# First batch's attention in halves of the tokens: turns, scores and softmax of two chunks of x while the other two land

## Chip, cores, metric

One core of one Trainium2 chip. The metric is the device time of the whole program in microseconds (us). A program on one core has no second core to compare states with; every run here was classed fast.

The profiles use short names: PE is TensorE (the array of products), PEld its weight loads, DVE VectorE, ACT ScalarE, POOL GpSimd, SP SyncE, which here issues transfers. L304 is line 304 of the kernel. The grant is the share of its full clock that the array is given. To turn a tile is to transpose it with a product on PE.

## The reference

Eight batches of a cross attention between 512 tokens and 32 state rows per head, then a feed-forward layer with the activation h * erf(softplus(h)) over 4608 rows in the reference's sizes (4352 come out: 8 x (512 + 32)).

```python
scores = scale * np.matmul(x, state.transpose(0, 1, 3, 2))     # x: 8,8,512,64  state: 8,8,32,64
scores = scores - scores.max(-1, keepdims=True)
a = np.exp(scores)
a /= a.sum(-1, keepdims=True) + 1e-09
xread = np.matmul(a, state)
# ... the same the other way round gives sread (32 rows a head); concatenated on the token axis
h = x2 @ w_in                                                  # 512 -> 2048
g = h * erf(np.maximum(h, 0.0) + np.log1p(np.exp(-np.abs(h))))
out = g @ w_out                                                # 2048 -> 512
```

Only the attention of batch 0, in the first 22 us, is touched by the change.

## The kernel before: the parts that matter

The transfers of the opening, in the order of their issue. Chunks 0 and 2 of x go out on ACT's queue, 1 and 3 on SP's; the state (`st`) follows on SP, then the first weights:

```python
x_t[0] = xin.tile([P, NC, H, D], F32, name="x")
for c in range(NC):
    (nc.scalar, nc.sync)[c % 2].dma_start(
        out=x_t[0][:, c], in_=x[0, :, P * c:P * c + P].rearrange("h p d -> p h d"))
for e in range(2):
    nc.sync.dma_start(out=st[:, 0, D * e:D * e + D],
                      in_=state[0].rearrange("(i e) n d -> e i n d", e=2)[e])
```

Dummy products keep the array busy (`warm`); `states` turns the state; instructions of each engine stay in the order in which they are written.

```python
def warm(n):
    for _ in range(n):
        last = nc.tensor.matmul(out=spare[:, 0:P], lhsT=ident, rhs=ident, start=True, stop=True)

# attention0, cut:
for c in 1, 0, 2, 3:
    if c == 2:
        warm(3)
    for i in range(NI):
        nc.tensor.transpose(out=xp[i][:, P * c:P * c + P],
                            in_=xt[:, c, 2 * i:2 * i + 2, :], identity=ident)
for i in range(NI):                       # all four chunks at once
    (nc.scalar.copy, nc.vector.tensor_copy)[i % 2](xT[:, i, :], xp[i])
states(range(1))
s2 = scored(0, xT)
between[0]()                              # warm(32), first weights on ACT
...
for e in range(2):                        # states_weights
    nc.vector.transpose(out=both[:, e], in_=sc[e])
for e in range(2):
    nc.vector.reduce_max(out=m1[:, e], in_=a[:, e], axis=AX.X)
for e in range(2):
    nc.vector.tensor_tensor(a[:, e], a[:, e], over(m1[:, e]), op=ALU.subtract)
    nc.scalar.activation(out=a[:, e], in_=a[:, e], func=ACTF.Exp, scale=scale)
# ... sums, conversion of the first weights (L147 to L149), normalise, transpose to aT, L703
```

Of the kernel before, what the change touches and what calls it, by code (L numbers as in the profile page):

```python
# [8 lines left out]
F32 = mybir.dt.float32  # L9
U32 = mybir.dt.uint32  # L10
ALU = mybir.AluOpType
ACTF = mybir.ActivationFunctionType
AX = mybir.AxisListType
# [3 lines left out]
def kernel(  # L17
# [17 lines left out]
    nc = tc.nc  # L35
    B, H, S, D = x.shape
    Ns = state.shape[2]
    d_model, d_ff = moe_w_in.shape
    P = 128
    NI = H // 2  # L40
    NC = S // P
# [5 lines left out]
    scale = 1.0 / (D ** 0.5)  # L47
# [4 lines left out]
    xin = ctx.enter_context(tc.tile_pool(name="xin", bufs=1))  # L52
    att = ctx.enter_context(tc.tile_pool(name="att", bufs=1))
    small = ctx.enter_context(tc.tile_pool(name="small", bufs=2))
    keep = ctx.enter_context(tc.tile_pool(name="keep", bufs=2))
# [3 lines left out]
    ps_at = ctx.enter_context(tc.tile_pool(name="ps_at", bufs=2, space=PSUM))  # L59
    ps_h = ctx.enter_context(tc.tile_pool(name="ps_h", bufs=2, space=PSUM))  # L60
    ps_o = ctx.enter_context(tc.tile_pool(name="ps_o", bufs=1, space=PSUM))

    ident = const.tile([P, P], F32, name="ident")
# [42 lines left out]
    st = const.tile([P, B, P], F32, name="st")  # L106
# [7 lines that stand above are left out]
# [52 lines left out]
    def warm(n):  # L166

        for _ in range(n):
            last = nc.tensor.matmul(out=spare[:, 0:P], lhsT=ident, rhs=ident, start=True,
                                    stop=True)  # L170
        return last
# [3 lines left out]
    aT = {}  # L175

    def states(bs):


        ps = ps_h.tile([P, len(bs), P], F32, name="h")  # L180
        for k, b in enumerate(bs):
            last = nc.tensor.transpose(out=ps[:, k], in_=st[:, b, :], identity=ident)
        nc.scalar.copy(st[:, bs[0]:bs[-1] + 1, :], ps)
        return last

    over = lambda t: t.unsqueeze(2).to_broadcast([P, NC * NI, Ns])
# [3 lines left out]
    def scored(b, xT):  # L190


        s2 = [ps_at.tile([P, S], F32, name="at") for _ in range(2)]
        for i in reversed(range(NI)):
            for e in range(2):
                r, q = slice(D * e, D * e + D), slice(Ns * i, Ns * i + Ns)
                on_pe = nc.tensor.matmul(out=s2[e][q, :], lhsT=st[r, b, q], rhs=xT[r, i, :],  # L197
                                         start=True, stop=True)
        marks.append(on_pe)
        return s2  # L200
# [10 lines left out]
    def states_weights(b, sc, both):  # L211

        aT[b] = keep.tile([P, 2, S], F32, name="aT")
        a = both[:, 0:2].rearrange("p e (k n) -> p e k n", n=Ns)
        m1 = small.tile([P, 2, NC * NI], F32, name="m1")
# [7 lines that stand above are left out]
        return a  # L223

    def sums(a):
        z1 = small.tile([P, 2, NC * NI], F32, name="z1")
        for e in range(2):
            nc.vector.reduce_sum(out=z1[:, e], in_=a[:, e], axis=AX.X)
        return z1

    def normalise(a, z1):
        nc.vector.tensor_scalar(z1, z1, 1e-9, None, op0=ALU.add)
        nc.vector.reciprocal(z1, z1)
        for e in range(2):
            nc.vector.tensor_tensor(a[:, e], a[:, e], over(z1[:, e]), op=ALU.mult)

    def largest(sc):
        m2 = small.tile([P, 2], F32, name="m2")
        for e in range(2):
            nc.vector.reduce_max(out=m2[:, e:e + 1], in_=sc[:, e], axis=AX.X)  # L240
        nc.vector.tensor_scalar(m2, m2, -scale, None, op0=ALU.mult)
        return m2

    def weigh_tokens(sc, m2, a2):

        z2 = small.tile([P, 2], F32, name="z2")
        for e in range(2):
            nc.scalar.activation(out=a2[:, e], in_=sc[:, e], func=ACTF.Exp, bias=m2[:, e:e + 1],
                                 scale=scale, accum_out=z2[:, e:e + 1])
        return z2  # L250

    def inverse(z):
        nc.vector.tensor_scalar(z, z, 1e-9, None, op0=ALU.add)
        nc.vector.reciprocal(z, z)

    def turn_weights(a2):
        a2T = att.tile([P, 2, NC, P], F32, name="sc")
        for e in range(2):
            ps = ps_at.tile([P, NC, P], F32, name="at")
            for c in range(NC):  # L260
                nc.tensor.transpose(out=ps[:, c, :], in_=a2[:, e, P * c:P * c + P],
                                    identity=ident)
            nc.scalar.copy(a2T[:, e], ps)
        return a2T
# [27 lines left out]
    def attention0(between):  # L292



        xt = x_t[0]
        xT = att.tile([P, NI, S], F32, name="xT")
        xp = [ps_o.tile([P, S], F32, name="o%d" % i) for i in range(3)]
        xp.append(ps_h.tile([P, S], F32, name="h"))
        for c in 1, 0, 2, 3:  # L300
            if c == 2:
                warm(3)
            for i in range(NI):
                nc.tensor.transpose(out=xp[i][:, P * c:P * c + P],  # L304
                                    in_=xt[:, c, 2 * i:2 * i + 2, :], identity=ident)
        for i in range(NI):
            (nc.scalar.copy, nc.vector.tensor_copy)[i % 2](xT[:, i, :], xp[i])
        states(range(1))
        s2 = scored(0, xT)
        between[0]()  # L310
        both = att.tile([P, NI, S], F32, name="xT")
        sc = att.tile([P, 2, S], F32, name="sc")
        a = states_weights(0, s2, both)
        for e in range(2):
            nc.scalar.copy(sc[:, e], s2[e])
        between[1]()
        z1 = sums(a)
        between[2]()
        normalise(a, z1)
        for e in range(2):  # L320
            nc.vector.transpose(out=aT[0][:, e], in_=both[:, e])

        def rest():
            a2 = both[:, 2:4]
            m2 = largest(sc)
            yield
            z2 = weigh_tokens(sc, m2, a2)
            inverse(z2)
            yield
            a2T = turn_weights(a2)  # L330
            yield
            read_tokens(0, a2T, z2)
            yield

        return rest()

    def turn_x(b):
        xT = att.tile([P, NI, S], F32, name="xT")
        last = nc.vector.transpose(out=xT.rearrange("p i t -> p (i t)"),
                                   in_=xq_t.pop(b).rearrange("p i m d -> p (i m d)"))  # L340
        if b + 1 < B:
            load_xq(b + 1)
        return xT, last
# [289 lines left out]
    def begins(b):  # L633
        return 1 - b % 2
# [44 lines left out]
    def fetch():  # L679
        if len(made) < len(pieces):  # L680
            kind, j = w = pieces[len(made)]
            made[w] = (weights_in if kind == "i" else weights_out)(j)

    def on_act(kind, j, ks=range(2)):
        for k in ks:
            made[kind, j][0][k]()

    def on_dve(kind, j, ks=range(3)):
        for k in ks:
            made[kind, j][1][k]()  # L690
            if k == 2:
                fetch()
# [25 lines left out]
    def group():  # L718
        return [act.tile([P, 4, S], F32, name=n) for n in ("s", "hs")]
# [3 lines left out]
        fetch()  # L723
    warm(8)

    def after_scores():
        warm(32)
        on_act("i", 0)

    def before_sums():  # L730
        on_act("i", 1)
        on_dve("i", 0, [0, 1])

    def amid_sums():
        on_dve("i", 0, [2])
        on_act("o", 0, [0])
        m_t[0, 0] = mix.tile([P, 2, gw], F32, name="m")
        mixed_part(0, 0, 0, 2, nc.scalar.copy, nc.scalar.copy)
        warm(5)

    rest = attention0((after_scores, before_sums, amid_sums))
    g0 = group()

    def some0(g, gT, rs, ts):
# [112 lines left out]
    xT, _ = turn_x(1)  # L857
# [7 lines left out]
    turn = attention(1, xT)  # L865
# [40 lines left out]
    at = [combine_a(1)]  # L906
# [12 lines left out]
    for b in range(1, B + 1):  # L919
# [4 lines left out]
        for g, (first, second) in enumerate(groups):  # L924
# [5 lines left out]
            if b + 1 < B:  # L930

                late = b == 1
                if g == late:
                    side[6 if late else 6] = (lambda: behind(marks, next, turn)) if late else \
                        lambda old=turn: (next(old), behind(marks, next, turn))
                    turn = attention(b + 1)
# [3 lines left out]
                if g > 1:  # L940
                    o = g - 2 ^ begins(b + 1)
# [56 lines left out]
```

## Time and profile before

| | before |
|---|---|
| time, median of 6 runs (range) | 734.82 us (734.64 to 735.06) |
| span of the profiled run, mean grant of the array's clock | 733.0 us, 0.999 |
| PE, DVE, ACT busy | 98%, 71%, 54% |
| first half transpose of the scores on DVE | 11.46 us |
| first L703 (first product with the attention weights) | 21.99 us |
| first projection | 30.87 us |

The last three rows are the ones to follow. The opening is a chain that ends in the first projection; after it PE works nearly without a gap. The prediction below shows the lines. What it doesn't show is the view of busy time by stretches: after the stretch and its length come the busy time of PE, PEld, DVE, ACT and POOL (with the number of instructions), the granted clock, the DMA share and GB/s. The kernel before, in two stretches of about 3.4 us that matter later:

```profile
4.70:8.15 3.45, 2.40 (x20) 1.98 (x19) 0.00 (x0) 0.00 (x0) 0.00 (x0) 1.00 1.27 252
8.15:11.55 3.40, 2.44 (x28) 1.24 (x26) 1.38 (x3) 1.30 (x4) 0.00 (x0) 1.00 1.05 393
```

PE is busy for 70% of the first and 72% of the second (2.40 of 3.45, 2.44 of 3.40), and the grant is full.

### The profile page before, as it was taken

To read this page: it belongs to the slowest core of one execution; us is meant where nothing else is said; L and a number is where in the kernel's file an instruction comes from. 1 tells how busy PE (TensorE), PEld (TensorE's weight loads), DVE (VectorE), ACT (ScalarE), POOL (GpSimd) and SP (SyncE) were. 2 spreads that over 40 slices of the span, in tenths; PEclk is the share of its full clock that TensorE was granted. 3 is DMA by queue.
4 is the path that set the end of the run, shared out by engine and by line. 5 is a ranking of instruction groups with operands and counts; after the bars stand their busy time and mean duration, and the time that the engine had idled before them with its cause. 6 is when DMAs were issued, how large, how long until landed. Compare 5 with 4: busy or idle time off the path is not lost.

```text
span 733.0 us, 12127 instructions
## 1 busy us (share of the span) xinstructions
PE 721.4 (98%) x5016; PEld 587.0 (80%) x5016; DVE 523.7 (71%) x765; ACT 397.0 (54%) x499; POOL 0.7 (0%) x6
## 2 busy tenths in 40 slices
PE   8899999999999999999999999999999999999998
PEld 7434435878889888988989888988898899999996
DVE  4987887998698666867587669866686756675423
ACT  4898894657455445754355445554565434443340
POOL 0000000000000000000000000000000000000000
PEclk9999999999999999999999999999999999999999
DMA  7587842331152201410061104220121000000001
GB/s 233 175 244 213 218 95 58 87 58 21 38 97 55 53 1 44 102 30 30 1 144 23 37 1 93 57 43 13 26 62 30 30 1 30 1 30 1 30 1 29
DMA packets 139166, 46.40 MB, mean 63 GB/s; under 512 B 126696, under 2 KB 130536, under 8 KB 139112
## 3 DMA queue, kind: packets, MB, share of 16 engines
q1 hardware_dynamic: 136840, 44.92, 24.7%
q10 hardware_dynamic: 2272, 0.72, 0.5%
q8 instruction: 39, 0.64, 0.4%
q14 instruction: 15, 0.12, 0.1%
HBM read 33.03 MB, written 8.91 MB: 57 GB/s over the span
## 4 chain that ended last, share of the span: by engine, by line
PE 87%; DVE 6%; ACT 2%; issue 1%; DMA 0%; SPq 0%; DVEq 0%; ACTq 0%
PE o L593 48%; PE h L487 26%; PE o L543 6%; PE at L401 2%; PE h L401 1%; PE h L703 1%; PE at L197 1%; PE at L415 1%; PE h L277 1%; DVE hs L495 1%; DVE raw L569 1%; DVE s L538 1%; DVE s L716 0%; DVE hs L710 0%; DMA out_dram<-ot 0%
## 5 line engine op out<-in xcount | busy, mean ns | idle before, releaser
L593 PE MATMUL o<-w_out,s 128*128 128x256 f32 x480 | 118.2, 380 | 0.9 <-DVE ot L603 0.5
L593 PE MATMUL o<-raw,hs 128*128 128x256 f32 x480 | 117.0, 382 | 0.0
L494 ACT ACTIVATE s<-hs 128x512 f32<-128x512 f32 x120 | 75.3, 630 | 76.1 <-DVE hs L495 75.7
L593 PE MATMUL o<-w_out,hs 128*128 128x256 f32 x480 | 114.0, 380 | 0.2 <-DVE hs L592 0.2
L593 PEld LDWEIGHTS o<-raw,hs 128*128 128x128 f32 x480 | 90.0, 190 | 22.5 <-issue 10.9
L495 DVE TENSOR_TENSOR hs<-hs,h 128x512 f32<-128x512 f32 x90 | 61.7, 686 | 63.7 <-PE h L487 63.7
L593 PEld LDWEIGHTS o<-w_out,hs 128*128 128x128 f32 x480 | 90.6, 190 | 16.8 <-issue 4.2
L593 PEld LDWEIGHTS o<-w_out,s 128*128 128x128 f32 x480 | 84.6, 191 | 9.2 <-DVE ot L603 0.7
L495 DVE TENSOR_TENSOR hs<-s,h 128x512 f32<-128x512 f32 x60 | 41.0, 683 | 68.9 <-PE h L487 68.4
L487 PEld LDWEIGHTS h<-aT,m 128*128 128x128 f32 x672 | 83.9, 192 | 4.7 <-issue 1.4
L487 PE MATMUL h<-aT,m 128*128 128x128 f32 x672 | 84.7, 275 | 0.2 <-ACT s L498 0.2
L538 DVE TENSOR_TENSOR s<-s,hs 128x2048 f32<-128x2048 f32 x30 | 68.5, 2284 | 19.9 <-ACT s L537 19.9
L498 ACT COPY s<-h 128x512 f32<-128x512 f32 x29 | 17.0, 585 | 113.3 <-PE h L487 113.3
L543 PE MATMUL o<-w_out,s 128*128 128x512 f32 x128 | 59.0, 600 | 0.6 <-DVE s L716 0.5
L487 PE MATMUL h<-sy,sx 128*128 128x128 f32 x448 | 59.1, 275 | 0.0
L503 ACT COPY hs<-h 128x512 f32<-128x512 f32 x29 | 17.0, 585 | 76.1 <-PE h L487 76.1
L487 PEld LDWEIGHTS h<-sy,sx 128*128 128x128 f32 x448 | 56.6, 192 | 1.8 <-issue 0.5
L537 ACT ACTIVATE s<-s 128x2048 f32<-128x2048 f32 x30 | 57.4, 1912 | 0.3
L593 PE MATMUL o<-raw,s 128*128 128x256 f32 x240 | 56.8, 379 | 0.0
L543 PEld LDWEIGHTS o<-w_out,s 128*128 128x128 f32 x128 | 23.1, 190 | 30.7 <-issue 25.8
L593 PEld LDWEIGHTS o<-raw,s 128*128 128x128 f32 x240 | 43.5, 190 | 4.8
L494 ACT ACT_TABLE_LOAD x31 | 39.8, 1283 | 0.5
(130 smaller groups left out, 912.0 us busy)
## 6 DMA issues: line engine op xcount, KB each, us to landing
raw<-in_moe_w_in_dram SPq DMA_DIRECT2D x8, 1024.0 KB, 5.6
raw<-in_moe_w_out_dram SPq DMA_DIRECT2D x8, 1024.0 KB, 4.9
xq<-in_x_dram SPq DMA_DIRECT2D x112, 64.0 KB, 2.2
x<-in_x_dram SPq DMA_DIRECT2D x56, 128.0 KB, 2.8
out_dram<-ot SPq DMA_DIRECT2D x18, 256.0 KB, 2.2
sc<-xT SPq DMA_DIRECT2D x112, 32.0 KB, 1.9
out_dram<-ot SPq DMA_DIRECT2D x28, 128.0 KB, 1.8
x<-in_x_dram SPq DMA_DIRECT2D x2, 256.0 KB, 5.0
```

The source lines that it names most:

```text
L197: on_pe = nc.tensor.matmul(out=s2[e][q, :], lhsT=st[r, b, q], rhs=xT[r, i, :], start=True, stop=True)
L277: nc.tensor.matmul(out=sr[q, e, :], lhsT=a2T[:, e, c, q], rhs=xt[:, c, 2 * i + e, :], start=(c == 0), stop=(c == NC - 1))
L401: nc.tensor.matmul(out=ps[k][e][q, :], lhsT=st[r, b, q], rhs=w_in[r, 2 * g:2 * g + 2, i, :], start=True, stop=True)
L487: last = nc.tensor.matmul(out=bank[:, q], lhsT=lhsT, rhs=rhs, start=(first and i == 0 and k == 0), stop=(i == GF - 1 and k == len(ops) - 1 ...
L494: nc.scalar.activation(out=s[:, k], in_=hs[:, k], func=ACTF.Softplus)
L495: add = lambda o, x, y: nc.vector.tensor_tensor(o, x, y, op=ALU.add)
L498: copy(m1, p)
L503: copy(c11, p)
L537: return (nc.scalar.activation(out=s, in_=s, func=ACTF.Erf), nc.vector.tensor_tensor(s, s, hs, op=ALU.mult))
L538: nc.vector.tensor_tensor(s, s, hs, op=ALU.mult))
L543: nc.tensor.matmul(out=acc[r], lhsT=gT[:, i, P * r:P * r + P], rhs=w_out[:, GF * g + i, :], start=(g == 0 and i == 0), stop=(g == NG - 1 a ...
L593: nc.tensor.matmul(out=acc[bank][:, E2 * c:E2 * c + E2], lhsT=lhs[:, i, :], rhs=rhs[:, g, i, :], start=(first and i == 0 and c == 0), stop ...
```

## The change

The intent: two chunks of x have landed by 5.4 us, the other two only by 7.8. Work in halves of 256 tokens, so that the turns, copies, scores and softmax of the first half run while the second half lands.

```diff
-        for c in 1, 0, 2, 3:
-            if c == 2:
-                warm(3)
-            ...                                # all turns, then all copies
-        states(range(1))
-        s2 = scored(0, xT)
-        between[0]()
-        a = states_weights(0, s2, both)
+        def exps(t):                           # turn, copies, score, ...: each for one half t
+            k = blocks[t]
+            nc.vector.reduce_max(out=m1[:, :, k], in_=a[:, :, k], axis=AX.X)
+            nc.vector.tensor_tensor(a[:, :, k], a[:, :, k], over(m1[:, :, k]), op=ALU.subtract)
+            nc.scalar.activation(out=a[:, :, k], in_=a[:, :, k], func=ACTF.Exp, scale=scale)
+        copies(0, turn(0))
+        states(range(1))
+        warm(1)
+        s0 = score(0)
+        xp = turn(1)
+        turn_scores(0, s0)
+        copy_scores(0, s0)
+        copies(1, xp)
+        warm(3)
+        s1 = score(1)
+        exps(0)
+        between[0]()                           # warm(28), half of the first weights on ACT
+        turn_scores(1, s1)
+        exps(1)
+        between[1]()
+        copy_scores(1, s1)
+        sum_(0)
+        between[2]()
+        sum_(1)
+        between[3]()                           # ..., warm(8)
```

The transfers stay as they were. The dummy products keep their total, in other places.

More of the change, by code (lines that the diff above doesn't have):

```diff
@@ L292, in attention0 @@
     def attention0(between):
+        H2 = S // 2
+        NB = NC * NI // 2
         xt = x_t[0]
-        xT = att.tile([P, NI, S], F32, name="xT")
-        xp = [ps_o.tile([P, S], F32, name="o%d" % i) for i in range(3)]
-        xp.append(ps_h.tile([P, S], F32, name="h"))
-        for c in 1, 0, 2, 3:
-            if c == 2:
-                warm(3)
-            for i in range(NI):
-                nc.tensor.transpose(out=xp[i][:, P * c:P * c + P],
-                                    in_=xt[:, c, 2 * i:2 * i + 2, :], identity=ident)
@@ L306, in attention0 @@
-        for i in range(NI):
-            (nc.scalar.copy, nc.vector.tensor_copy)[i % 2](xT[:, i, :], xp[i])
-        states(range(1))
-        s2 = scored(0, xT)
-        between[0]()
+        xT = xin.tile([P, NI, S // Ns, Ns], F32, name="xq").rearrange("p i m n -> p i (m n)")
         both = att.tile([P, NI, S], F32, name="xT")
         sc = att.tile([P, 2, S], F32, name="sc")
-        a = states_weights(0, s2, both)
-        for e in range(2):
-            nc.scalar.copy(sc[:, e], s2[e])
+        aT[0] = keep.tile([P, 2, S], F32, name="aT")
@@ new lines, in attention0, with turn @@
+        a = both[:, 0:2].rearrange("p e (k n) -> p e k n", n=Ns)
+        m1, z1 = (small.tile([P, 2, NC * NI], F32, name=n) for n in ("m1", "z1"))
+        cols = [slice(H2 * t, H2 * t + H2) for t in range(2)]
+        blocks = [slice(NB * t, NB * t + NB) for t in range(2)]
+        over = lambda v: v.unsqueeze(3).to_broadcast([P, 2, NB, Ns])
+        def turn(t):
+            xp = [ps_o.tile([P, 2, H2], F32, name="o%d" % (2 * t)),
+                  ps_h.tile([P, 2, H2], F32, name="h") if t else
+                  ps_o.tile([P, 2, H2], F32, name="o1")]
+            for c in ((1, 0), (2, 3))[t]:
+                for i in range(NI):
+                    nc.tensor.transpose(out=xp[i // 2][:, i % 2, P * (c % 2):P * (c % 2) + P],
+                                        in_=xt[:, c, 2 * i:2 * i + 2, :], identity=ident)
+            return xp
@@ new lines, in copies, with score @@
+        def copies(t, xp):
+            nc.scalar.copy(xT[:, 0:2, cols[t]], xp[0])
+            nc.vector.tensor_copy(xT[:, 2:4, cols[t]], xp[1])
+        def score(t):
+            s2 = [ps_at.tile([P, S], F32, name="at")[:, 0:H2] for _ in range(2)]
+            for i in range(NI):
+                for e in range(2):
+                    r, q = slice(D * e, D * e + D), slice(Ns * i, Ns * i + Ns)
+                    nc.tensor.matmul(out=s2[e][q, :], lhsT=st[r, 0, q], rhs=xT[r, i, cols[t]],
+                                     start=True, stop=True)
+            return s2
@@ new lines, in turn_scores, with copy_scores @@
+        def turn_scores(t, s2):
+            for e in range(2):
+                nc.vector.transpose(out=both[:, e, cols[t]], in_=s2[e])
+        def copy_scores(t, s2):
+            for e in range(2):
+                nc.scalar.copy(sc[:, e, cols[t]], s2[e])
+        def exps(t):
[3 more added lines that the diff above has]
+            nc.scalar.activation(out=a[:, :, k], in_=a[:, :, k], func=ACTF.Exp, scale=scale)
@@ L316, in attention0, with sum_ @@
+        def sum_(t):
+            nc.vector.reduce_sum(out=z1[:, :, blocks[t]], in_=a[:, :, blocks[t]], axis=AX.X)
+        copies(0, turn(0))
[12 more added lines that the diff above has]
+        exps(1)
         between[1]()
-        z1 = sums(a)
+        copy_scores(1, s1)
@@ L724, with amid_scores, amid_exps, amid_sums @@
     warm(8)
-    def after_scores():
-        warm(32)
-        on_act("i", 0)
-    def before_sums():
+    def amid_scores():
+        warm(28)
+        on_act("i", 0, [0])
+    def amid_exps():
+        on_act("i", 0, [1])
+    def amid_sums():
+        on_dve("i", 0, [0])
+    def behind_sums():
         on_act("i", 1)
-        on_dve("i", 0, [0, 1])
-    def amid_sums():
-        on_dve("i", 0, [2])
+        on_dve("i", 0, [1, 2])
         on_act("o", 0, [0])
@@ L738, in amid_sums @@
         mixed_part(0, 0, 0, 2, nc.scalar.copy, nc.scalar.copy)
-        warm(5)
-    rest = attention0((after_scores, before_sums, amid_sums))
+        warm(8)
+    rest = attention0((amid_scores, amid_exps, amid_sums, behind_sums))
     g0 = group()
```

## The prediction

> **What bounds the kernel now.** I read the page first, for what binds the whole span; then the chain of work that ended last, in order of time, for where the opening joins it; then the timeline of the first 31 us, because the change touches nothing later. The page:
>
> ```profile
> PE 721.4 (98%) x5016; PEld 587.0 (80%) x5016; DVE 523.7 (71%) x765; ACT 397.0 (54%) x499; POOL 0.7 (0%) x6
> PE 87%; DVE 6%; ACT 2%; issue 1%; DMA 0%; SPq 0%; DVEq 0%; ACTq 0%
> ```
>
> TensorE is the bound of the span as a whole, but its 98% includes the dummy products of the opening (line L169, which only keep the array busy). So the opening is not measured by PE's digits; the question is when the first useful, unbroken PE work may begin. The chain of the window from 0 to 31.2 us ends so:
>
> ```profile
> 26.82 1.13 DVE w_out L148
> 27.95 0.60 DVE hs L710
> 28.55 0.06 DVE w_out L149
> 28.61 0.99 issue
> 29.60 1.23 DVE s L716
> 30.83 0.04 issue
> 30.87 0.70 PE o L543
> ```
>
> At 30.87 us the first projection starts, and what released it is VectorE (DVE). From there PE is nearly gapless (14.0 us of the 14.0 between 31 and 45 in the table of busy time by stretches), so a shift of that start should pass to the end about one to one. Before it, this is the timeline:
>
> ```profile
> 1.86 1.59 SPq L112 DMA_DIRECT2D st<-in_state_dram  x2
> 4.84 0.51 PE L304 MATMUL o<-ident,x 128*128 128x128 f32 x3
> 5.87 0.27 PE L304 MATMUL h<-ident,x 128*128 128x128 f32 x1
> 7.84 0.55 PE L304 MATMUL o<-ident,x 128*128 128x128 f32 x3 [1.03 <-DMA x<-in_x_dram]
> 8.65 0.27 PE L304 MATMUL h<-ident,x 128*128 128x128 f32 x1
> 8.75 0.69 DVE L307 COPY xT<-o 128x512 f32<-128x512 f32 x1 [8.75 <-PE o L304]
> 9.24 0.30 PE L182 MATMUL h<-ident,st 128*128 128x128 f32 x1 [0.31 <-DMA st<-in_state_dram]
> 9.36 0.68 DVE L307 COPY xT<-h 128x512 f32<-128x512 f32 x1
> 9.60 0.28 ACT L183 COPY st<-h 128x128 f32<-128x128 f32 x1
> 10.18 1.09 PE L197 MATMUL at<-xT,st 64*32 64x512 f32 x16 [0.65 <-DVE xT L307]
> 11.46 1.31 DVE L217 STREAM_TRANSPOSE xT<-at 128x512 f32<-128x512 f32 x2 [1.42 <-PE at L197]
> 12.70 1.24 DVE L219 TENSOR_REDUCE m<-xT 128x16 f32<-128x512 f32 x2
> 19.93 1.29 DVE L235 TENSOR_TENSOR xT<-xT,z 128x512 f32<-128x512 f32 x2
> 21.99 3.67 PE L703 MATMUL h<-aT,m 128*128 128x512 f32 x8 [0.33 <-DVE aT L321]
> ```
>
> The reader should see three things. The first two chunks of x are turned by 6.1 us; the others by 8.9. DVE has no gap from 11.46 to about 31: its sum of work after the scores sets the first projection. And, decisive for me, the turn of the **state** (L182) waits for its own transfer, which is issued behind the x chunks of its queue. The record of landings in the trace says when: the chunks of x are complete at 4.76, 5.44, 7.17 and 7.79 us, the two halves of the state at 8.52 and 9.10. The state is the last input of the scores to arrive, not the first.
>
> **What the Trainium skill says.** "DMA: Bandwidth & Descriptors", section "Queues, rings and completion order": on each DMA engine descriptors are taken in ring order. The trace agrees as far as it can: the state, issued behind two chunks on one queue, landed last. "VectorE: DVE Perf Modes", section "The TRN2 errata": a vector operation pays a fixed cost, so cutting one in two pays it twice. Here two transposes of 512 columns start 0.64 us apart and the two copies 0.61; with 0.533 us for 512 columns at the page's 0.96 GHz, an estimate of some 0.07 us is fixed. "TensorE: Matmul & The Clock Gate", section "Part 1: The HAM clock gate": the array falls to half rate after an idle window of about 3.4 us, and rises after a busy one. The trace agrees on the rise: the first dummy products start 213 ns apart, those after 4.8 us 112 ns apart. No run yet shows the fall.
>
> **The change, part by part.**
> 1. Turning in halves. The copies of the first half (one 512-column operation each on ACT and DVE) can run at 6.0 to 6.9 us, where DVE idles now. That takes one of the two DVE copies (0.61 us) out of the row 8.75 to 10.04.
> 2. But in PE's program order the state's turn comes next, before the scores of half 0 and before the turns of half 1. PE works in order, so it stands from 6.14 until the state has landed: turn at 9.24, ACT copy 9.60 to 9.88, as now. The scores of half 0 then start at about 9.96 (now 10.18; that start waited 0.65 us for the second DVE copy, which no longer stands before it). So of all the overlap intended, 0.22 us comes out.
> 3. Scores of 256 columns: the sixteen passes of L415 with 256 columns take 0.66 to 0.79 us; end at 10.63. DVE can start its two half transposes at 10.75 (it took 0.1 to 0.2 after PE's end), each 0.33 us by the estimate above: until 11.42.
> 4. The turns of half 1, which could have run at 7.8 to 8.7 as now, wait in order behind these scores: eight at 0.109 us apart from 10.56, last end 11.60. DVE's copy of them, 11.64 to 12.25 (start to next start), now lies **after** the first transposes. Scores of half 1: 12.45 to 13.15, hidden under DVE.
> 5. DVE from 12.25: maximum and difference of half 0 (0.58 + 0.60) until 13.43, transposes of half 1 0.67, maximum and difference 1.18, to 15.28. Now the same place in the sequence (L147 can start) is 15.05, and it was reached without the copy. Then sum 0.60, L147 0.60, sum 0.60, L148 from about 17.25 (after a small wait for ACT), 1.14, L149 1.13, the two small operations 0.60: the product with 1/z starts at about 20.12, now 19.93. I have saved 0.2 us there because L148 no longer follows L147 directly (that pair starts 0.81 us apart now, other neighbours 0.60).
>    Check by sums: gained 0.71 us of earlier start (11.46 to 10.75) and that 0.2; lost 0.61 of copy, 0.22 waiting for it, 0.09 for two more transposes, some 0.17 waiting for L146 on ACT. Net loss about 0.2 us.
> 6. ACT: its two operations on the first weights are pushed between and behind the exponentials, so L146 ends near 17.1 (now 13.7), the second pair near 19.7 and L144 of w_out near 20.8 (now 19.9). The m copies follow at 20.8 to 21.4 (now 20.4 to 21.06), still before aT is done: hidden.
> 7. Dummy products: 8+3+32+5 become 8+1+3+28+8, the same total. The last eight take 16 passes of 0.1115 us = 1.78 from 20.46, so till 22.25, when aT's first half is ready at 22.05: the first L703 starts at 22.2 to 22.3, against 21.99.
>
> Sum: everything from L703 to the first projection moves back by 0.2 to 0.3 us. 734.76 + 0.25 = **735.0 us**.
>
> **Rivals.**
> (a) The intended gain: if the scores of half 0 ran at about 7 us, half 0's transposes, maximum and difference (1.85 us) would lie in DVE's idle time before 9.4, and the end would come 1 to 1.5 us earlier, some 733.5. Against it stands the landing record: the change moves no transfer. It needs the state nearly 2 us sooner than in the trace. A lesser form: DVE's order packs better than I think, and 0.3 to 0.5 us are gained (734.3). For it speaks that 0.2 us of the step between L147 and L148 was found only by looking; more such gaps may close.
> (b) The array goes cold: the dummy products between the chunks are gone, so PE is idle from 6.14 to 9.24, 3.1 us. If the gate falls, the scores, the turns and the second scores, all now in DVE's path, run at half rate: an estimate of 0.7 + 0.8 + 0.5 = 2 us at worst, 736 to 736.5. Against it: 3.1 us is short of 3.4, and products run at both edges of the gap. I give it one in ten.
> (c) ACT as the bound: the exponential of half 0 waits for nobody, but L146, pushed behind the second exponential, releases L148. Were ACT 0.5 us later than I think, DVE would stand, and the loss would be 0.6 to 0.8 us (735.5).
>
> **Range and chances.** The whole opening of DVE work that the change can reach is 3 us, 0.4% of the span, so neither side of 2% (14.7 us) is in reach of any rival. The middle is 735.0; a better packing gives 734.3, ACT or a cooled array 735.6 to 736. The three runs before spread 0.4 us. I take 734.2 to 735.9. Faster by over 2%: 0.003; slower: 0.007.
>
> **What would show it.** Right: the L182 successor still waits for the state's transfer and starts near 9.2; PE is idle from 6.1 to then; the first half transpose starts on DVE at 10.6 to 10.9; DVE's x copy of half 1 at 11.6; the product with 1/z at 20.0 to 20.3; the first L703 at 22.1 to 22.4, the first projection at 31.0 to 31.2. The step of in-order waiting is wrong if half 0's scores start before 9 us. The hidden ACT step is wrong if DVE idles over 0.3 us before L148. The clock step is wrong if passes after 9.2 us are 213 ns apart. The one-to-one step is wrong if the first projection moves by 0.2 and the end by something else.

## The result, and the profile after

The changed kernel takes 736.74 us (736.24 to 737.17, 6 runs), 1.9 us more than the 734.82 of the kernel before; the ratio is 1.0026, with a 95% interval of 1.0013 to 1.0038. (Ratios here are the mean time of one kernel's fast runs over the mean of the other's in the same rounds, so not quite the ratio of the medians quoted.) Every run lies above the predicted range of 734.2 to 735.9. The spread, 0.9 us, is twice that of before.

The timeline of the changed kernel, line by line against the one shown of before (L315 are the turns, now of two chunks each; L328 the scores; L334 the transposes; L321 DVE's copies of x; L753 is the old L703):

```profile
4.93 1.92 PE L315 MATMUL o<-ident,x 128*128 128x128 f32 x8
6.89 0.69 DVE L321 COPY xq<-o 128x512 f32<-128x512 f32 x1 [6.89 <-PE o L315]
8.85 0.31 PE L182 MATMUL h<-ident,st 128*128 128x128 f32 x1 [2.00 <-DMA st<-in_state_dram]
9.51 0.67 PE L328 MATMUL at<-xq,st 64*32 64x256 f32 x16
10.26 0.78 DVE L334 STREAM_TRANSPOSE xT<-at 128x256 f32<-128x256 f32 x2 [2.68 <-PE at L328]
...
11.40 0.63 PE L315 MATMUL h<-ident,x 128*128 128x128 f32 x2
...
12.07 0.69 DVE L321 COPY xq<-h 128x512 f32<-128x512 f32 x1 [1.03 <-PE h L315]
...
21.14 1.29 DVE L235 TENSOR_TENSOR xT<-xT,z 128x512 f32<-128x512 f32 x2
...
23.26 3.62 PE L753 MATMUL h<-aT,m 128*128 128x512 f32 x8
```

The state's turn indeed waits for its transfer, 2.00 us, with PE standing: the overlap is gone as predicted. But then the second turns take 1.93 us, from 10.10 to the last end at 12.03, not 1.04 (10.56 to 11.60 in the prediction): they start 0.213 us apart, the rate of the cold array. The stretches say why:

```profile
6.80:10.20 3.40, 1.27 (x21) 0.65 (x21) 0.69 (x1) 0.51 (x2) 0.00 (x0) 1.00 1.07 362
10.20:13.60 3.40, 3.40 (x22) 3.04 (x30) 2.28 (x5) 1.29 (x3) 0.00 (x0) 0.50 1.05 417
13.60:22.00 8.40, 8.12 (x93) 7.17 (x78) 8.15 (x14) 7.25 (x11) 0.00 (x0) 1.00 0.24 69
```

The grant (the third number from the right) is 0.50 for one stretch of 3.41 us, 10.20 to 13.62 in the trace's record of the clock, right after a stretch of the same length in which PE was busy for only 1.27 us. So DVE's second copy waits 1.03 us. The other five runs left no trace, but each run's mean grant is on record: 0.995 to 0.998 in the six runs of the changed kernel, 0.999 or 1.0 in every run of the kernel before for which it is listed. One stretch of 3.41 us at half the clock takes 0.0023 off the mean over 734.5 us (an estimate from these two lengths), so the grants fit at least one such fall in every run. The end of the chain before the first projection has the same links as before, later:

```profile
30.82 1.27 DVE s L766
32.09 0.04 issue
32.14 0.70 PE o L593
```

The first projection starts 1.27 us later than before; the span is 1.5 us longer (734.5 against 733.0; this run took 736.28 us in the timing).

### The profile page after: what moved, and what is told of

Read it like the earlier page. It is cut to its first block, busy times and chain, and to the rows that moved or that the text cites. A ratio compares the mean times of both kernels' runs of the same rounds, so it can differ in the third digit from the quotient of the medians.

```text
span 734.5 us, 12160 instructions
## 1 busy us (share of the span) xinstructions
PE 723.5 (99%) x5032; PEld 589.2 (80%) x5032; DVE 524.7 (71%) x767; ACT 397.3 (54%) x501; POOL 0.7 (0%) x6
## 4 chain that ended last, share of the span: by engine, by line
PE 86%; DVE 5%; ACT 3%; issue 1%; DVEq 0%; ACTq 0%
PE o L643 48%; PE h L537 26%; PE o L593 5%; PE at L451 2%; PE h L451 1%; PE h L753 1%; PE at L197 1%; PE h L277 1%; PE at L465 1%; ACT raw L146 1%; DVE raw L619 1%; DVE hs L545 1%; ACT L763 1%; DVE s L588 1%; DVE hs L760 0%
```

## The experiments

Theory 1: the gap in front of the state's turn lets the clock fall, and that is most of the loss. Theory 2: order, pieces and dependent neighbours on DVE lose it, the clock is beside the point. Beyond both: is the overlap worth anything if the state comes early? Twelve kernels ran, all correct against the reference.

| run | built on | median us (range) | ratio to before (95%) |
|---|---|---|---|
| a_fill | changed | 735.45 (735.28 to 735.79) | 1.0009 (0.9996 to 1.0021) |
| b_nofill | before | 735.72 (734.99 to 736.14) | 1.0013 (0.9999 to 1.0027) |
| a_st | changed | 737.65 (737.32 to 737.87) | 1.0037 (1.0025 to 1.0050) |
| b_st | before | 739.88 (738.73 to 740.72) | 1.0066 (1.0053 to 1.0079) |
| a_st2 | changed | 734.22 (734.08 to 735.40) | 0.9991 (0.9977 to 1.0004) |
| a_st2x | changed | 734.12 (734.03 to 735.59) | 0.9994 (0.9980 to 1.0007) |
| b_dep | before | 735.14 (734.93 to 735.27) | 1.0003 (0.9989 to 1.0016) |
| b_st2 | before | 735.23 (735.05 to 735.36) | 1.0004 (0.9990 to 1.0018) |
| a_turns | changed | 734.90 (734.72 to 735.11) | 1.0000 (0.9987 to 1.0012) |
| a_st3x | changed | 733.05 (732.95 to 733.19) | 0.9975 (0.9961 to 0.9988) |
| a_st2xf | changed | 734.27 (734.07 to 734.31) | 0.9990 (0.9977 to 1.0004) |
| b_st3 | before | 734.75 (734.61 to 734.80) | 0.9998 (0.9984 to 1.0011) |

The kernel before gave medians of 734.82 to 734.93 in all rounds. Intervals that include 1 leave effects of a few tenths of a microsecond to the traces.

### a_fill: the gap filled

```diff
         copies(0, turn(0))
+        warm(9)
         states(range(1))
```

> The changed kernel with nine more dummy products between the turn of the first two chunks and the turn of the state, so that PE isn't idle from 6.7 to 8.8 us. Theory 1 (the clock: the gap lets the grant fall to 0.5 for one window, 10.2 to 13.6 us in the changed kernel's profile, and the second turns at 213 ns and the second scores lie in DVE's path): the grant never falls after its first rise, the second turns are 110 ns apart, DVE's second copy of x starts near 11.2 instead of 12.07, the first L753 near 22.2 instead of 23.26; time about 735.2 us, 1.5 less than the changed kernel. Theory 2 (the loss is the order on PE and DVE's dependent pairs, the clock is beside the point): no change beyond 0.3 us, 736.4 to 736.9.

Measured: 735.45 us, 1.3 less than the changed kernel. The grant stays at 1.0 from 4.81 us to the end. Its timeline:

```profile
9.12 0.30 PE L182 MATMUL h<-ident,st 128*128 128x128 f32 x1 [1.05 <-DMA st<-in_state_dram]
11.50 0.69 DVE L321 COPY xq<-h 128x512 f32<-128x512 f32 x1 [0.19 <-PE h L315]
...
20.42 1.29 DVE L235 TENSOR_TENSOR xT<-xT,z 128x512 f32<-128x512 f32 x2
...
22.54 3.61 PE L754 MATMUL h<-aT,m 128*128 128x512 f32 x8
```

DVE's second copy waits 0.19 us instead of 1.03, although the state landed later here, and the first L754 comes at 22.54 against 23.26. All five runs have mean grants of 0.999 or 1.0. Theory 1 holds for 1.3 of the 1.9 us. Some 0.6 us remain against before, with the clock full: theory 2's part, more than the 0.25 predicted.

Two stretches at the end of this run matter for the account of the clock below, 1.53 us of work and then none, both at the full grant:

```profile
728.43:731.85 3.42, 1.53 (x8) 1.00 (x6) 1.28 (x3) 0.00 (x0) 0.00 (x0) 1.00 0.48 136
731.85:733.66 1.81, 0.00 (x0) 0.00 (x0) 0.00 (x0) 0.00 (x0) 0.00 (x0) 1.00 0.12 34
```

### b_nofill: the filler taken out of the kernel before

```diff
         for c in 1, 0, 2, 3:
-            if c == 2:
-                warm(3)
             for i in range(NI):
```

> The kernel before without its three dummy products between the turns of chunk 0 and chunk 2: the one gap-filler that the change took out at that place, taken out alone. Theory 1: the window before the scores is then judged idle in some executions too; the grant falls and the turns or scores run at half rate; time 0.5 to 1.5 us over before, and a wider spread than 0.4 us. Theory 2: same as before within 0.2 us, grant 1.0 throughout after the rise.

Measured: 735.72 us, with one run at 734.99 and four at 735.65 to 736.14. The one profiled is the 734.99, and its grant held:

```profile
5.70:9.10 3.40, 1.68 (x15) 1.38 (x13) 0.11 (x1) 0.22 (x1) 0.00 (x0) 1.00 1.17 300
```

No trace of the slower four was kept, but their mean grants are on record: 0.995 to 0.998, against 1.0 in the profiled run. So the clock fell in the four slower runs and not in the fast one, though where in the run it fell is not shown. Taken out alone, the filler raises the median by 0.9 us; the interval of the ratio just includes 1.

### a_st and b_st: the state ahead of the second chunk of each queue

```diff
     for c in range(NC):
-        (nc.scalar, nc.sync)[c % 2].dma_start(...)
-    for e in range(2):
-        nc.sync.dma_start(out=st[:, 0, D * e:D * e + D], ...[e])
+        queue = (nc.scalar, nc.sync)[c % 2]
+        queue.dma_start(...)
+        if c < 2:
+            queue.dma_start(out=st[:, 0, D * c:D * c + D], ...[c])
```

> The changed kernel with the two transfers of the state issued behind the first chunk of each queue instead of behind both. The state should land near 5 to 6 us, with chunks 2 and 3 a little later (8 us). If the late state is what takes the overlap away, the scores of half 0 start near 7 us, DVE's first half transposes near 8, PE has no gap over 1.5 us and the grant stays; DVE then finishes the first half's transposes before 9 us and its second copy near 9 to 9.5; the first L753 near 20.5 to 21; time 733.3 to 734.3, below before. If the overlap is worth nothing in itself (DVE's dependent pairs and smaller pieces eat it), time 735 to 736.5.

> Control: the kernel before with the same order of transfers. Its scores wait for all four chunks, so an early state saves at most the 0.15 us between the state's copy and the last copy of x, less what chunks 2 and 3 land later: 734.6 to 735.2 by both theories.

Both missed, and in the same way. The state did land at 6.27 us, and half 0's transposes began at 8.15. But chunk 2 came at 11.40:

```profile
11.44 0.69 PE L316 MATMUL o<-ident,x 128*128 128x128 f32 x2 [3.35 <-DMA x<-in_x_dram]
```

Its issue on ACT's queue had slipped from 1.26 to 2.43 us, just ahead of the first weights on SP's queue (2.75), and it landed behind the first of those (complete at 10.68). The unsplit kernel, which needs all four chunks for any score, lost more (5.1 us against 2.8). In both the clock fell too (from 9.79 and 10.29 us, for two and three stretches of 3.41 us). The experiment moved two things at once and couldn't judge the early state; a_st2 and a_st3x were made for that.

### a_st2, a_st2x and the control b_st2: all of x still ahead of the weights

```diff
     for c in range(NC):
         (nc.scalar, nc.sync)[c % 2].dma_start(...)
-    for e in range(2):
-        nc.sync.dma_start(out=st[...], ...)
+        if c == 1:
+            for e in range(2):
+                nc.sync.dma_start(out=st[...], ...)
```

and in a_st2x, besides:

```diff
         copy_scores(0, s0)
+        maxima(0)                 # reduce_max of half 0, taken out of exps(0)
         copies(1, xp)
-        warm(3)
+        warm(5)
```

> The changed kernel with the state issued on SP between chunk 1 and chunk 3 (in a_st chunk 2 went behind the first weights, because its issue on the scalar queue came late; here all of x still stands ahead of the weights on its own queue). State complete near 6 us, chunks 2 and 3 near 8. Theory A (what spoils the change is that the scores of half 0 can't start before the state, and PE's gap with it): scores of half 0 near 7.2 us, second turns near 8.1 with no DMA wait over 1 us, DVE's second copy near 9.3, product with 1/z near 18.3, first L753 near 20.5; time 733.2 to 733.8, 1 to 1.6 below before. Theory B (only the clock mattered): time as a_fill, 735.2 to 735.8. If the grant still falls for a window, 734 to 735.

> As a_st2, with half 0's maximum put ahead of DVE's second copy of x (so that DVE doesn't wait for the second turns, and the difference doesn't follow its own maximum directly) and two more dummy products before the second scores. If dependent neighbours on DVE cost what the changed kernel's trace shows (maximum to difference 0.71 us start to start, against 0.60 for independent neighbours), 0.1 to 0.4 us below a_st2; else the same.

> Control for a_st2: the kernel before with its state issued between chunks 1 and 3. Its scores still wait for all of x; gain at most 0.15 us, loss by chunk 3 landing later at most some 0.3 us: 734.6 to 735.2, grant 1.0 throughout.

Measured: 734.22, 734.12 and 735.23 us. The state was complete at 7.89 and 7.53 us in the profiled runs of the two changed kernels, not at 6 (its first half came at 6.12 and 5.96, the second, issued behind it, 1.6 to 1.8 us later; why so much later was not traced), and the gain is 0.7 and 0.8 instead of 1 to 1.6 us. The control's median is 0.3 higher, with chunk 3 landing at 8.4, but its interval includes 1. Theory B (the clock alone) is out: both are below a_fill by over a microsecond. a_st2's profiled run happened to be its slowest, 735.40, and in it the grant fell once more, 9.10 to 12.51, after

```profile
5.70:9.10 3.40, 1.58 (x25) 0.94 (x23) 0.69 (x1) 0.85 (x2) 0.00 (x0) 1.00 1.17 301
```

So one and the same kernel has executions with and without the fall: the other four runs of a_st2 have mean grants of 0.999 or 1.0 and times of 734.08 to 734.50. a_st2x has the same split, three runs at 0.999 and one at 0.996, its slowest (735.59). Moving the maximum ahead of the copy can't be told from noise in the time (734.22 and 734.12).

### b_dep: dependent neighbours on DVE, alone

```diff
-        for e in range(2):
-            nc.vector.reduce_max(out=m1[:, e], in_=a[:, e], axis=AX.X)
         for e in range(2):
+            nc.vector.reduce_max(out=m1[:, e], in_=a[:, e], axis=AX.X)     # for batch 0
             nc.vector.tensor_tensor(a[:, e], a[:, e], over(m1[:, e]), op=ALU.subtract)
```

(Shown for batch 0; in the run the other batches keep their order.)

> The kernel before with the first batch's maxima and differences in the order max 0, difference 0, max 1, difference 1, so each difference follows the maximum that it needs directly, as in the changed kernel; same operations, same number. If a dependent neighbour costs 0.10 to 0.12 us more than an independent one, the product with 1/z comes 0.2 to 0.3 us later than 19.93 (two such pairs, less one at the seam), the first L703 too, and the time is 735.0 to 735.1. If the wait is hidden in the 0.60 between neighbours, 734.8 as before.

```profile
12.93 0.64 DVE L222 TENSOR_REDUCE m<-xT 128x16 f32<-128x512 f32 x1
13.61 0.69 DVE L223 TENSOR_TENSOR xT<-xT,m 128x512 f32<-128x512 f32 x1
14.22 0.68 DVE L222 TENSOR_REDUCE m<-xT 128x16 f32<-128x512 f32 x1
14.93 0.69 DVE L223 TENSOR_TENSOR xT<-xT,m 128x512 f32<-128x512 f32 x1
```

From a maximum to the difference that needs it, 0.68 and 0.71 us start to start; from a difference to the maximum behind it, which needs nothing of it, 0.61. Before, with two maxima and then two differences, all steps were 0.57 to 0.60. The way from the first transpose to the product with 1/z is 8.72 us, 8.47 before: 0.25 more for the same operations, as expected. (The product itself starts 0.48 us later than before, at 20.41; the other 0.23 were there before the first transpose.) The time, 735.14 us, points the same way but its interval includes 1; the claim rests on the trace.

### a_turns: PE's order alone

```diff
         copies(0, turn(0))
+        warm(3)
+        copies(1, turn(1))
         states(range(1))
         warm(1)
         s0 = score(0)
-        xp = turn(1)
         turn_scores(0, s0)
         copy_scores(0, s0)
-        copies(1, xp)
         warm(3)
```

> The changed kernel with PE's order alone changed and no transfer moved: the turns of chunks 2 and 3 stand ahead of the state's turn (with three dummy products between the pairs, as in the kernel before), their copies too; scores, transposes and softmax stay in halves. If the changed kernel loses because its second turns and copy stand behind the late state and in a cold clock, this removes both: second copy of x on DVE done by 9.7, scores of half 0 near 9.8, first L753 within 0.3 of 21.99 us, time 734.5 to 735.1, grant 1.0 throughout after the rise. If halves in themselves cost more (pieces, dependent pairs), 735.2 to 735.8.

Measured: 734.90 us, ratio 1.0000, grant full from 6.33 us on. The first L753 is where it was before:

```profile
10.69 0.78 DVE L334 STREAM_TRANSPOSE xT<-at 128x256 f32<-128x256 f32 x2 [0.99 <-PE at L328]
...
19.82 1.29 DVE L235 TENSOR_TENSOR xT<-xT,z 128x512 f32<-128x512 f32 x2
...
21.93 1.47 PE L753 MATMUL h<-aT,m 128*128 128x512 f32 x3
```

So with the second turns in front of the late state, the whole 1.9 us are back, and halves neither gain nor lose: DVE's transposes start 0.77 us before those of the kernel before (10.69 against 11.46), and the way from there to the product with 1/z, with its extra pieces and dependent neighbours, is 0.66 us longer (9.13 against 8.47). This also says what the 0.6 us left in a_fill are. a_fill has the same pieces and the same dependent neighbours, but its second copy stands in DVE's row behind the transposes: the copy takes 0.61 us there and 0.16 of waiting, and the start is 0.17 earlier (10.53), so the product comes 0.60 us later than in a_turns.

### a_st3x, its control b_st3, and a_st2xf

a_st3x is a_st2x with another order of transfers; b_st3 is the kernel before with that order; a_st2xf is a_st2x with `warm(4)` in front of `states`.

```diff
+    chunk(nc.scalar, 0)
+    chunk(nc.sync, 1)
+    half_state(nc.scalar, 1)
+    half_state(nc.sync, 0)
+    chunk(nc.sync, 2)
+    chunk(nc.sync, 3)
```

> The changed kernel with half 0's maximum ahead of the second copy of x, and the state issued behind one chunk on each queue as in a_st, but chunk 2 moved to SP ahead of chunk 3, so that all of x stands ahead of the weights on one queue. State complete near 6.3 us, chunks 2 and 3 by 8.2; no PE gap over 1.2 us; scores of half 0 near 7.2, product with 1/z near 17.9 to 18.3, first L753 near 20.1; time 732.9 to 733.5, the fastest, spread under 0.6 us as the array never idles long. If chunks 2 and 3 land late on one queue (after 9 us), the gain shrinks to that of a_st2x, 734.1.

> Control for a_st3x: the kernel before, unsplit, with the transfers in the order of a_st3x. If the gain of a_st3x (1.8 us) is the halves' own, made possible by the early state, this one stays at 734.6 to 735.3, as its scores still wait for all four chunks. If it is the order of the transfers alone, it gains too, 733 to 734.

> a_st2x with four dummy products between the first turns and the state's turn (0.9 us warm, 1.7 cold). If the slow outliers of a_st2 and a_st2x (735.4, 735.6) are executions in which the clock fell, they go: all runs within 0.5 us, median 734.0 to 734.3. If they are something else, they stay.

Measured: a_st3x 733.05 us, the fastest of all and 1.8 us below the kernel before (its interval ends at 0.9988). The state is complete at 6.16 us, chunks 2 and 3 at 7.24 and 7.98:

```profile
6.33 0.27 PE L190 MATMUL h<-ident,st 128*128 128x128 f32 x1
7.12 0.79 PE L336 MATMUL at<-xq,st 64*32 64x256 f32 x16 [0.29 <-ACT st L191]
7.96 0.78 DVE L342 STREAM_TRANSPOSE xT<-at 128x256 f32<-128x256 f32 x2 [0.74 <-PE at L336]
...
19.92 3.62 PE L767 MATMUL h<-aT,m 128*128 128x512 f32 x8
```

The state's turn has no wait in front of it any more, DVE begins the transposes 3.5 us before the old kernel, and the first L767 comes 2.1 us earlier. The control, with the same transfers and no halves, stays at 734.75: the order of the transfers gives nothing without the halves, and the halves nothing without the order. a_st2xf has all four runs within 734.07 to 734.31 and a full grant from 4.87 us: the outlier of a_st2x doesn't appear. Four runs don't prove it gone, but with a_st2's profiled outlier and the grant of 0.996 in a_st2x's own, the clock is its likely cause.

## Why the prediction was wrong

The direction was right, the size was not: 0.25 us of loss was forecast, 1.9 came. By its own steps:

- **The chain and the one-to-one step: right but for a few tenths.** In a_fill the first projection moves by 0.54 and the span by 0.7 us; in a_st3x by -2.10 and -1.8; in the changed kernel by 1.27 and 1.5. Where the remainder of 0.1 to 0.3 comes from was not traced.
- **Step 2, the state holds PE: right.** PE waits for the state's transfer, and half 0's scores start at 9.51 (9.96 predicted; the state landed 0.4 us sooner in that run, at 8.71). a_turns and a_st3x show it from both sides.
- **Rival (b), the clock: the step that failed.** The prediction dismissed the fall with "3.1 us is short of 3.4, and products run at both edges" and gave it one in ten; its own sign of the error, passes 213 ns apart after 9.2 us, is what came. The real gap was even shorter, 2.00 us, and the grant fell all the same. That idle time is the cause is shown from both sides: a_fill fills the gap and no run falls, b_nofill takes a filler out and four of five fall.

  The longest gap is not what decides: with 1.69 us (a_st2) the grant fell, with 1.72 (b_nofill) and 1.88 (the end of a_fill) it held. The work in a fixed stretch of 3.41 us orders the runs better: in the opening the grant fell after stretches with 0.69 (b_st), 1.27 (changed), 1.45 (a_st) and 1.58 us of PE work (a_st2), and held after 1.68 (b_nofill) and after 2.16 or more. But it held after the 1.53 us at the end of a_fill, so busy time as the profile counts it doesn't settle it either. The stretches that fell in the changed kernel, a_st and a_st2 include score passes on a part of the array (64x32); whether these count for less was not tested.

  In the kernel before the stretch had 2.40 us, of which the three dummy products taken out are 0.83. The price: second turns at 0.213 instead of 0.109 us apart, in DVE's path, about 0.7 us at L753 between the profiled runs of a_fill and the changed kernel (which take 735.45 and 736.28 us), 1.3 us in the medians. The size given for rival (b), 736 to 736.5, was a little short; its chance was wrong.
- **Step 5, DVE's sum: a term mis-sized.** From the first transpose to the product with 1/z the prediction has 9.37 us (10.75 to 20.12), a_fill 9.90. The excess of 0.53 is: two dependent steps of 0.71 where 0.58 was put (0.26), the second pair of half transposes with the step to the maximum 0.81 where 0.67 was put (0.14; the two halves start 0.37 apart, not 0.33 as estimated), and L149 right behind L148, on which it depends, 1.26 where 1.14 was put (0.12). (A later copy, 0.08 more, and most of the wait put for L146, 0.11 less, nearly cancel.) The prediction took every step's length from a kernel whose neighbours were independent. b_dep shows the first of these by itself. The saving of 0.2 us where L148 no longer follows L147 was real.
- **Step 6, ACT hidden: right.** DVE waits less than 0.1 us for L146 (the step from the second sum to L148 is 0.65 to 0.67 us, against 0.60), and the m copies are done at 21.64 in a_fill, 0.9 us before they are needed.
- **Rival (a), the intended gain: right as a condition.** It was priced at 733.5 if the state came 2 us sooner; a_st3x, with the state at 6.16 instead of 8.7 to 9.1, takes 733.05 (with half 0's maximum and the fillers moved as well).

The loss, then: about 1.3 us to the clock and about 0.6 us to the order in DVE's row, where the second copy comes behind the transposes and the head start of the halves no longer pays for pieces and dependent neighbours. The gain that was intended, 1.8 us in a_st3x, needs the state early. What makes the changed kernel's runs spread over 0.9 us is probably the phase of the clock's stretches (the rise came at 4.73 us in the profile of before and at 6.79 in the other), but only one of its runs was profiled. What exactly the clock counts in a stretch, and whether the limit is sharp, stays open.

## What to carry to other kernels

Before work is split so as to overlap a transfer, list when each of its inputs lands: the last one, here a small operand behind large ones in its queue, decides, and in-order engines make everything behind it wait too. Fillers between bursts are part of a schedule; when they go, count the array's work in every 3.4 us and don't go by the longest gap alone: with gaps of 2.00 and 1.69 us the grant was lost here. And when the pieces of a chain get fewer per kind, dependent operations become neighbours: take their step from a pair that depends.

## What the Trainium skill lacked or had wrong

- "TensorE: Matmul & The Clock Gate", section "Why this matters for your kernels", warns of idle gaps over some 3 us. Here the longest gap was 2.00 us in the changed kernel and 1.69 in a_st2, and the grant fell to 0.50 for 3.41 us. The page has the length of the window right, in its section "Part 1: The HAM clock gate" (10.20 to 13.62 us here), but not how much work in it keeps the clock: windows with up to 1.58 us of busy PE lost it, others with 1.68 (b_nofill) and 1.53 (the end of a_fill) kept it. And a window of 2.57 us of work at half rate did not raise the grant in b_st, one of 3.40 did.
- The same page, section "Part 4: PE-mode transpose", says that transposes don't count as busy in the same way. In b_nofill a window with nothing but transposes, 1.68 us of them, kept the full grant, and in the changed kernel the grant rose at 6.79 us, when the 1.86 us just before were turns. The profile shows the turns as products and doesn't say whether a transpose mode was on.
- "VectorE: DVE Perf Modes", section "The DRAIN you can't avoid", finds a semaphore between operations to cost nothing. For operations that don't depend on each other that fits; a 512-column difference right behind its own maximum started 0.68 to 0.71 us after it (0.03 to 0.04 after its end), independent neighbours 0.57 to 0.61 (b_dep and the kernel before). The page lacks this figure.
